# Equal FFN column groups, and gate logits through DRAM, in a fused attention and expert kernel

## The chip, the cores and the metric

The kernel runs on one core of one Trainium2 chip. The metric is the device time of one execution in microseconds (us). Each version was run several times. A profiled execution also gives a trace, whose span (first to last instruction) is some 1.7 us shorter than the time of the same execution. Engine names in the profile: PE is TensorE, PEld its weight loads, DVE VectorE, ACT ScalarE, POOL GpSimd, SP SyncE; SPq is SyncE issuing DMAs.

## The reference, cut to what matters

x is 2048 tokens of 1024, in bf16. Branch A is a linear attention of 32 heads with phi(t) = max(t, 0) + min(exp(t), 1), up to a tiny constant. Branch B adds a gated FFN's output to one token, the one with the highest router score. Both are mixed by a gate per token.

```python
x = A_x
g = sigmoid((x * gate_w).sum(-1, keepdims=True))    # one gate per token
a = linear_attention(x, wqkv) @ wo                  # branch A
r = x @ w_r
i = argmax(r)                                       # one token of 2048
y = (silu(x[i] @ w_gate) * (x[i] @ w_up)) @ w_down  # F = 3584 units
b = x;  b[i] += y * sigmoid(r[i])                   # branch B
return g * a + (1 - g) * b
```

## The kernel before

The main loop, for token tiles 4 to 15, makes keys and values (`unit_KV`), accumulates them (`unit_KVACC`) and makes queries (`unit_Q`). These units, all but the accumulation, go through the same four buffers (`ps_work`) in PSUM, the memory that TensorE writes to. ScalarE and VectorE empty (evacuate) keys and queries by `phi_evac`; values are copied out by ScalarE. The router runs before this loop, and the FFN's pieces are spread over it.

One matmul group gives router scores and gate logits of all tokens, one row of each per block of 512 tokens. `rg_f` is its copy in SBUF: gate logits in partitions 1, 33, 65 and 97. Two steps of the loop matter here: four small matmuls (eight records in the trace) move the logits to token columns, and the FFN's 3584 columns are made in halves of four and three groups of 512, each in its own 32 columns of the TensorE array.

```python
ps_work = ctx.enter_context(tc.tile_pool(name="ps_work", bufs=4, space=PSUM))
# issued on SyncE, in this order, ahead of the loop
nc.sync.dma_start(out=wq[:], in_=wqkv_v[:, :, 0:D])
nc.sync.dma_start(out=xp[:], in_=x2d)       # copy of x in DRAM; row i is overwritten later
# ...
def phi_evac(ps, out_ap):
    e0 = tmp.tile([P, 512], F32, tag="phi_e0")
    last_act[0] = nc.scalar.activation(e0[:], ps, ACTF.Exp)
    e1 = tmp.tile([P, 512], F32, tag="phi_e1")
    nc.vector.tensor_scalar(e1[:], e0[:], 1.0, EPS, op0=ALU.min, op1=ALU.add)
    nc.vector.scalar_tensor_tensor(out_ap, ps, 0.0, e1[:], op0=ALU.max, op1=ALU.add)
# ...
rg_f = rt.tile([P, 512], F32)
nc.scalar.copy(rg_f[:], rps[:])
# ... VectorE finds the candidates of the four blocks: cand
nc.gpsimd.dma_start(out=c4[:], in_=cand[0:128:32, :])            # "c" in the trace
# ... VectorE reduces c4 to the token's index: idx_f, idx_i
nc.gpsimd.dma_start(out=xsel_row[:], in_=x2d[bass.ds(idx_val, 1), :])

def router_part2():                          # called at t == 5
    # ... eight matmuls xs_ps <- xsel_row
    gl_ps = ps_ffn.tile([P, NT], F32, tag="f")
    for b in range(4):
        nc.tensor.matmul(gl_ps[:, 4 * b : 4 * b + 4], lhsT=rg_f[:, b * P : (b + 1) * P], rhs=selg[:], start=True, stop=True)
    nc.scalar.activation(gate[...], gl_ps[...], ACTF.Exp, scale=-1.0)
    # ... gate = 1 / (1 + gate), omg = 1 - gate
# ... ffn_pieces, for each half, matrix and c (8 chunks of 128 rows)
wt = ffw.tile([P, 2048], BF, tag="ffw")      # ten of these in flight
nc.sync.dma_start(out=wt[:, 0 : 512 * nr], in_=wv[:, c, c0 : c0 + 512 * nr])
for j in range(nr):                          # nr = 4, then 3
    nc.tensor.matmul(ps[32 * j : 32 * j + 32, :], lhsT=xs_pad[:, c, :], rhs=wt[:, 512 * j : 512 * j + 512],
                     start=(c == 0), stop=(c == KC - 1), tile_position=(0, 32 * j))
```

`pin_act`, which the kernel uses at two other places, adds an ordering-only dependency on the latest evacuation, so that the scheduler can't move an operation ahead of it on ScalarE.

Of the kernel before, what the change touches and what calls it, by code (L numbers as in the profile page):

```python
# [11 lines left out]
F32 = mybir.dt.float32  # L12
I32 = mybir.dt.int32
U32 = mybir.dt.uint32
ALU = mybir.AluOpType
ACTF = mybir.ActivationFunctionType
# [3 lines left out]
P = 128  # L20
# [3 lines left out]
NT = S // P  # L24
# [11 lines left out]
def kernel(  # L36
# [13 lines left out]
    nc = tc.nc  # L50
# [5 lines left out]
    const = ctx.enter_context(tc.tile_pool(name="const", bufs=1))  # L56
    keep = ctx.enter_context(tc.tile_pool(name="keep", bufs=1))
    dram = ctx.enter_context(tc.tile_pool(name="dram", bufs=1, space=DRAM))
    ps_work = ctx.enter_context(tc.tile_pool(name="ps_work", bufs=4, space=PSUM))
    ps_ffn = ctx.enter_context(tc.tile_pool(name="ps_ffn", bufs=1, space=PSUM))  # L60

    pq_all = keep.tile([P, NG, S], BF)
    gate = keep.tile([P, NT], F32)
    omg = keep.tile([P, NT], F32)
# [59 lines left out]
    nc.gpsimd.memset(one_bf[:], 1.0)  # L124
    sel4 = const.tile([P, 4], BF)
    nc.gpsimd.memset(sel4[:], 0.0)
    selg = const.tile([P, 4], F32)
    nc.gpsimd.memset(selg[:], 0.0)
    for j in range(4):
        nc.gpsimd.memset(sel4[32 * j : 32 * j + 1, j : j + 1], 1.0)  # L130
    pidx_i = const.tile([P, 4], I32)
    nc.gpsimd.iota(pidx_i[:], pattern=[[-32, 4]], base=-1, channel_multiplier=1)
    pidx_f = const.tile([P, 4], F32)
    nc.vector.tensor_copy(pidx_f[:], pidx_i[:])
    nc.vector.tensor_scalar(selg[:], pidx_f[:], 0.0, None, op0=ALU.is_equal)
    off16_i = const.tile([P, 1], I32)
    nc.gpsimd.iota(off16_i[:], pattern=[[0, 1]], base=0, channel_multiplier=16)
    off16 = const.tile([P, 1], F32)
# [3 lines left out]
    xs_pad = rt.tile([P, KC, 32], BF)  # L142
# [98 lines left out]
    nc.vector.tensor_copy(r_bf[:], rps[:])  # L241
    rg_f = rt.tile([P, 512], F32)
    nc.scalar.copy(rg_f[:], rps[:])
    r_f = rt.tile([P, 512], F32)
    nc.vector.tensor_copy(r_f[:], r_bf[:])
    mx8 = rt.tile([P, 8], F32)
# [27 lines left out]
    def router_part3():  # L274
        pin_act(nc.scalar.activation(sig[:], sig[:], ACTF.Exp, scale=-1.0))
        nc.vector.tensor_scalar_add(sig[:], sig[:], 1.0)
        nc.vector.reciprocal(sig[:], sig[:])

    def router_part2():
        xs_ps = ps_ffn.tile([P, KC], F32, tag="f")  # L280
        for c in range(KC):
            nc.tensor.matmul(xs_ps[:, c : c + 1], lhsT=xsel_row[0:1, c * P : (c + 1) * P], rhs=one_bf[0:1, 0:1],
                             start=True, stop=True)
        nc.vector.tensor_copy(xs_pad[:, :, 0], xs_ps[:])
        gl_ps = ps_ffn.tile([P, NT], F32, tag="f")
        for b in range(4):
            nc.tensor.matmul(gl_ps[:, 4 * b : 4 * b + 4], lhsT=rg_f[:, b * P : (b + 1) * P], rhs=selg[:], start=True, stop=True)  # L287
        nc.scalar.activation(gate[:].rearrange("p (j b) -> p j b", b=4), gl_ps[:].rearrange("p (b j) -> p j b", j=4),
                             ACTF.Exp, scale=-1.0)
        nc.vector.tensor_scalar_add(gate[:], gate[:], 1.0)  # L290
        nc.vector.reciprocal(gate[:], gate[:])
        nc.vector.tensor_scalar(omg[:], gate[:], -1.0, 1.0, op0=ALU.mult, op1=ALU.add)


    ffw = ph1.enter_context(tc.tile_pool(name="ffw", bufs=FFN_DEPTH))
    h_bf = [rt.tile([P, 512], BF, name=f"h_bf{i}") for i in range(2)]
    sg_t = [rt.tile([P, 512], F32, name=f"sg{i}") for i in range(2)]
# [1 line left out]

    def ffn_pieces():  # L300
        for half in range(2):
            nr = 4 if half == 0 else 3
            c0 = 2048 * half
            for wi, wmat in enumerate((B_w_gate, B_w_up)):
                wv = wmat.rearrange("(c p) f -> p c f", p=P)
                for c in range(KC):
                    def load(half=half, nr=nr, c0=c0, wv=wv, c=c):
                        wt = ffw.tile([P, 2048], BF, tag="ffw")
                        nc.sync.dma_start(out=wt[:, 0 : 512 * nr], in_=wv[:, c, c0 : c0 + 512 * nr])
                        return wt  # L310

                    def compute(wt, half=half, nr=nr, wi=wi, c=c):
                        if c == 0:
                            ps = ps_ffn.tile([P, 512], F32, tag="f")
                            ffn_state["ps"] = ps
                            if nr < 4:
                                nc.vector.memset(ps[96:128, :], 0.0)
                        ps = ffn_state["ps"]
                        for j in range(nr):
                            nc.tensor.matmul(ps[32 * j : 32 * j + 32, :], lhsT=xs_pad[:, c, :], rhs=wt[:, 512 * j : 512 * j + 512],  # L320
                                             start=(c == 0), stop=(c == KC - 1), tile_position=(0, 32 * j))
                        if c == KC - 1:
                            if wi == 0:
                                eg = tmp.tile([P, 512], F32, tag="ffn_e", bufs=1)
                                nc.scalar.activation(eg[:], ps[:], ACTF.Exp, scale=-1.0)
                                nc.vector.tensor_scalar_add(eg[:], eg[:], 1.0)
                                nc.vector.reciprocal(eg[:], eg[:])
                                nc.vector.tensor_tensor(sg_t[half][:], ps[:], eg[:], op=ALU.mult)
                            else:
                                nc.vector.tensor_tensor(h_bf[half][:], ps[:], sg_t[half][:], op=ALU.mult)  # L330

                                def h_transpose(half=half, nr=nr):
                                    hps = ps_ffn.tile([P, 16], F32, tag="f")
                                    for b in range(4):
                                        nc.tensor.matmul(hps[:, 4 * b : 4 * b + 4], lhsT=h_bf[half][:, b * P : (b + 1) * P],
                                                         rhs=sel4[:], start=True, stop=True)
                                    dst = hT_pad[:, 16 * half : 16 * half + 4 * nr, 0].rearrange("p (j b) -> p j b", b=4)
                                    src = hps[:].rearrange("p (b j) -> p j b", j=4)[:, 0:nr, :]
                                    nc.vector.tensor_copy(dst, src)

                                ffn_state["pending"] = h_transpose
                                ffn_state["barrier"] = True

                    yield load, compute
        wdv = B_w_down.rearrange("(k p) n -> p k n", p=P)
        for k2 in range(14):
            def load(k2=k2):
                wt = ffw.tile([P, 2048], BF, tag="ffw")
                nc.sync.dma_start(out=wt[:].rearrange("p (k n) -> p k n", k=2), in_=wdv[:, 2 * k2 : 2 * k2 + 2, :])
                return wt  # L350

            def compute(wt, k2=k2):
                if k2 == 0:
                    ffn_state["ps"] = ps_ffn.tile([P, 256], F32, tag="f", name="yps")
                ps = ffn_state["ps"]
                for kk in range(2):
                    k = 2 * k2 + kk
                    for j in range(4):
                        nc.tensor.matmul(ps[32 * j : 32 * j + 32, :], lhsT=hT_pad[:, k, :],  # L359
                                         rhs=wt[:, 1024 * kk + 256 * j : 1024 * kk + 256 * j + 256],  # L360
                                         start=(k == 0), stop=(k == 27), tile_position=(0, 32 * j))
                if k2 == 13:
                    brow = rt.tile([P, 256], BF, name="brow")
                    nc.vector.scalar_tensor_tensor(brow[:], ps[:], sig[:, 0:1], xsel4[:], op0=ALU.mult, op1=ALU.add)  # L364
                    nc.gpsimd.dma_start(out=xp[bass.ds(idx_val, 1), :].rearrange("o (j n) -> (o j) n", j=4),  # L365
                                        in_=brow[0:128:32, :])

            yield load, compute
# [4 lines left out]
    def ffn_prefetch():  # L373
        while len(inflight) < FFN_DEPTH:
            nxt = next(pieces, None)
            if nxt is None:
                return
            inflight.append((nxt[0](), nxt[1]))
# [16 lines left out]
                return  # L395

    ffn_prefetch()

    q_units = deque((g, j) for j in range(4) for g in range(NG))
    for t in range(4):  # L400
        unit_KVACC(t)
    for t in range(4, NT):
        for nb in range(4):
            unit_KV(t, nb)
            if nb == 1 and t > 4:
                unit_KVACC(t - 1)
        nq = Q_PER_T[t]
        for _ in range(nq):
            unit_Q(*q_units.popleft())
        if t == 5:  # L410
            router_part2()
        if t == 8:
            router_part3()
        if t >= 6:
            ffn_step(FFN_PER_T[t])
    unit_Q(*q_units.popleft())
# [145 lines left out]
```

## Time and profile before

| | before |
|---|---|
| median of 3 runs (range) | 267.6 us (267.37 to 267.88) |
| span of the profiled execution | 267.3 us |
| TensorE busy | 255.7 us, 96% |
| DMA moved | 47.71 MB, 33058 packets |
| SyncE: first FFN load issued, last issued | 30.68, 52.93 us |

The page's first lines stand in the prediction below. Two more views say what TensorE's time is made of. First the shares of the chain that ended last, from the page; then two rows of the groups of instructions, by form (line, engine, operation, tiles, shape, count, then busy us and mean ns of one, then idle time before them):

```profile
PE 77%; DVE 12%; DMA 7%; issue 2%; ACT 0%; POOL 0%; SPq 0%; DVEq 0%
```

```profile
L287 PE MATMUL gl_ps<-selg,rg_f 128*128 128x4 f32 x8 | 1.0, 253 | 0.1
L320 PE MATMUL ps<-wt,xs_pad 128*32 128x512 bf16 x112 | 7.6, 380 | 0.0
```

The chain is mostly TensorE. The two rows hold nearly all the TensorE work that the change touches. The second row also shows why means mislead: 112 matmuls of 380 ns would be 42.6 us, but three or four run beside each other and the group is busy for 7.6.

### The profile page before, as it was taken

Reading aid. Unit: us, or ns where it says so; the run is one execution under the profiler, and the core shown is the slowest. Engines: PE = TensorE matmul, PEld = TensorE weight load, DVE = VectorE, ACT = ScalarE, POOL = GpSimd, SP = SyncE. Lnnn points to the kernel's source line nnn. Section 1 sums busy time; section 2 is a strip of 40 time slices with the busy share of each in tenths; the row PEclk is TensorE's granted clock in tenths of the full one; section 3 lists DMA queues with packets and bytes.
Section 4 is the critical chain, followed back from the end, with each engine's and each line's share of the span. In section 5 each row is a group of like instructions: output and inputs, shape, how many; then the busy total and the mean of one; then the engine's idle time right before and its main releaser. Section 6 shows DMA issues by size and latency. Waiting matters only on the chain.

```text
span 267.3 us, 3972 instructions
## 1 busy us (share of the span) xinstructions
PE 255.7 (96%) x1510; PEld 121.8 (46%) x1537; DVE 144.5 (54%) x278; ACT 89.3 (33%) x138; POOL 50.3 (19%) x102
## 2 busy tenths in 40 slices
PE   7799999599999999999999999999999899999994
PEld 4444455245444445444444455544444344444443
DVE  4355014452375533539433425279999889984443
ACT  1433332123233322332322331233576623333310
POOL 7000001120000000000000000111969317990000
PEclk9999999999999999999999999999999999999999
DMA  6999998892078048019319608084000336455222
GB/s 228 359 312 220 246 521 306 292 415 93 0 259 333 1 154 316 4 45 348 120 36 357 238 0 300 17 286 168 1 1 2 125 100 197 150 170 177 86 78 78
DMA packets 33058, 47.71 MB, mean 178 GB/s; under 512 B 14152, under 2 KB 18640, under 8 KB 32976
## 3 DMA queue, kind: packets, MB, share of 16 engines
q1 hardware_dynamic: 32688, 47.32, 53.0%
q8 instruction: 12, 0.20, 0.3%
q0 software_dynamic: 320, 0.14, 0.2%
q14 instruction: 6, 0.05, 0.0%
q10 hardware_dynamic: 32, 0.00, 0.0%
HBM read 39.85 MB, written 8.39 MB: 180 GB/s over the span
## 4 chain that ended last, share of the span: by engine, by line
PE 77%; DVE 12%; DMA 7%; issue 2%; ACT 0%; POOL 0%; SPq 0%; DVEq 0%
PE ps L195 39%; PE ps L519 19%; PE ps L211 11%; DVE rb L476 4%; DVE e L169 3%; DMA c<-cand 3%; PE ps L320 3%; DVE pq_all L170 2%; DMA wkv<-in_A_wqkv_dram 2%; PE kvacc L204 2%; DMA rdp<-rd 1%; PE yps L359 1%; PE rps L237 1%; PE dps L453 1%; PE gl_ps L287 0%
## 5 line engine op out<-in xcount | busy, mean ns | idle before, releaser
L195 PE MATMUL ps<-wkv,xT 128*128 128x512 bf16 x498 | 113.9, 379 | 2.2 <-DMA wkv<-in_A_wqkv_dram 1.0
L195 PEld LDWEIGHTS <-xT 128*128 128x128 bf16 x512 | 48.8, 98 | 58.4 <-issue 2.9
L167 ACT ACTIVATE e<-ps 128x512 f32<-128x512 f32 x64 | 38.2, 597 | 81.7 <-PE ps L195 43.3
L169 DVE TENSOR_SCALAR e<-e 128x512 f32<-128x512 f32 x64 | 31.4, 492 | 55.7 <-ACT e L167 55.5
L211 PE MATMUL ps<-xT,wq 128*128 128x512 bf16 x248 | 58.3, 379 | 3.3 <-DVE idx_i L265 2.8
L519 PE MATMUL ps<-m_sb,pq_all 128*128 128x512 bf16 (+1 forms) x259 | 55.3, 372 | 1.0 <-DVE pq_all L170 0.6
L211 PEld LDWEIGHTS <-wq 128*128 128x128 bf16 x256 | 24.8, 98 | 33.6 <-issue 4.6
L519 PEld LDWEIGHTS <-pq_all 128*128 128x128 bf16 x264 | 25.7, 98 | 31.3 <-issue 1.8
L478 POOL TENSOR_TENSOR pq_all<-pq_all,rb 128x512 bf16<-128x512 bf16 x32 | 37.3, 1197 | 9.9 <-DVE rb L476 9.8
L200 ACT CAST vt<-ps 128x512 bf16<-128x512 f32 x32 | 18.8, 587 | 41.5 <-PE ps L195 41.5
L521 DVE SCALAR_TENSOR_TENSOR ot<-ps,gate,xg 128x512 bf16<-128x512 f32 (+1 forms) x33 | 23.8, 734 | 14.2 <-PE ps L519 14.1
L513 ACT ACTIVATE xg<-xt,omg 128x1024 f32<-128x1024 bf16 x16 | 18.2, 1151 | 29.7 <-DVE ot L521 25.0
L476 DVE STREAM_SHUFFLE rb<-rdp 128x512 f32<-128x512 f32 x32 | 22.7, 743 | 0.0
L170 DVE SCALAR_TENSOR_TENSOR pk<-ps,e 128x512 bf16<-128x512 f32 x32 | 22.1, 691 | 1.1
L170 DVE SCALAR_TENSOR_TENSOR pq_all<-ps,e 128x512 bf16<-128x512 f32 x32 | 21.8, 683 | 0.6
L192 POOL MEMSET vt<- 128x8 bf16 x16 | 1.9, 135 | 106.4 <-PE kvacc L204 106.4
L204 PEld LDWEIGHTS <-pk 128*128 128x128 bf16 x128 | 8.5, 98 | 3.3 <-issue 0.4
L204 PE MATMUL kvacc<-vt,pk 128*128 128x129 bf16 x128 | 9.7, 221 | 0.0
L484 ACT CAST m_sb<-ps 128x512 bf16<-128x512 f32 x16 | 8.6, 593 | 0.0
L458 DVE RECIPROCAL rd<-dn 128x512 f32<-128x512 f32 x2 | 6.7, 3353 | 3.2 <-ACT dn L456 3.2
L241 DVE CAST r_bf<-rps 128x512 bf16<-128x512 f32 x1 | 0.7, 691 | 13.9 <-PE rps L237 13.9
L365 POOL DMA_DIRECT2D xp<-brow x1 | 0.6, 575 | 38.5 <-DVE brow L364 38.5
(97 smaller groups left out, 87.0 us busy)
## 6 DMA issues: line engine op xcount, KB each, us to landing
wt<-in_B_w_down_dram SPq DMA_DIRECT2D x14, 512.0 KB, 9.2
wkv<-in_A_wqkv_dram SPq DMA_DIRECT2D x4, 1024.0 KB, 10.6
wt<-in_B_w_gate_dram SPq DMA_DIRECT2D x8, 512.0 KB, 21.6
wt<-in_B_w_up_dram SPq DMA_DIRECT2D x8, 512.0 KB, 8.1
xt<-xp SPq DMA_DIRECT2D x16, 256.0 KB, 2.7
out_dram<-ot SPq DMA_DIRECT2D x15, 256.0 KB, 2.0
wt<-in_B_w_gate_dram SPq DMA_DIRECT2D x8, 384.0 KB, 6.2
wt<-in_B_w_up_dram SPq DMA_DIRECT2D x8, 384.0 KB, 6.8
```

What stands on the lines that cost most here:

```text
L167: last_act[0] = nc.scalar.activation(e0[:], ps, ACTF.Exp)
L169: nc.vector.tensor_scalar(e1[:], e0[:], 1.0, EPS, op0=ALU.min, op1=ALU.add)
L170: nc.vector.scalar_tensor_tensor(out_ap, ps, 0.0, e1[:], op0=ALU.max, op1=ALU.add)
L195: nc.tensor.matmul(ps[:], lhsT=xT[:, c, t * P : (t + 1) * P], rhs=wkv[:, c, 512 * nb : 512 * nb + 512], start=(c == 0), stop=(c == KC - 1))
L200: nc.scalar.copy(vt_t[t][:, 4 * (nb - 2) : 4 * (nb - 2) + 4, 0:128], ps[:].rearrange("p (g e) -> p g e", g=4))
L204: nc.tensor.matmul(kv_slot(g), lhsT=pk_t[t][:, g * P : (g + 1) * P], rhs=vt_t[t][:, g, :], start=False, stop=False, skip_group_check=True)
L211: nc.tensor.matmul(ps[:], lhsT=wq[:, c, g * P : (g + 1) * P], rhs=xT[:, c, 512 * j : 512 * j + 512], start=(c == 0), stop=(c == KC - 1))
L476: nc.vector.stream_shuffle(rb[:], rd[:], [8 * (j % 2) + g] * 32)
L478: nc.gpsimd.tensor_tensor(sl, sl, rb[:], op=ALU.mult)
L513: pin_act(nc.scalar.activation(xg[:], xt[:], ACTF.Copy, scale=omg[:, t : t + 1]))
L519: nc.tensor.matmul(ps[:, 0:cw], lhsT=pq_all[:, g, t * P : (t + 1) * P], rhs=m_sb[:, g, c0 : c0 + cw], start=(g == 0), stop=(g == NG - 1))
L521: nc.vector.scalar_tensor_tensor(ot[:, c0 : c0 + cw], ps[:, 0:cw], gate[:, t : t + 1], xg[:, c0 : c0 + cw], op0=ALU.mult, op1=ALU.add)
```

## The change

It has two aims: equal FFN groups, so that the second half doesn't leave a quarter of the array's columns unused, and no TensorE work for the gate logits. 3584 columns become four groups of 896 = 512 + 384. The logits are written to DRAM as four rows of 2 KB and read back as 2048 single elements, token by token, into the columns where they are needed. The source calls the gate computation at tile 10 rather than at tile 5.

```diff
+    gl_d = dram.tile([4, 512], F32, name="gl_d")
+    gl = rt.tile([P, NT], F32)
+    def gate_logits():                       # called after the first ten FFN loads
+        nc.sync.dma_start(out=gl_d[:], in_=rg_f[1:128:32, :])
+        with nc.allow_non_contiguous_dma(reason="2048 gate logits to token columns"):
+            nc.sync.dma_start(out=gl[:].rearrange("p (j b) -> p j b", b=4), in_=gl_d[:].rearrange("j (b p) -> p j b", p=P))
+    def gates():                             # called at t == 10
+        nc.scalar.activation(gate[:], gl[:], ACTF.Exp, scale=-1.0)
+        nc.vector.tensor_scalar_add(gate[:], gate[:], 1.0)
 ... (reciprocal and 1 - gate as before; selg, gl_ps and their set-up removed)
-            nr = 4 if half == 0 else 3
-            c0 = 2048 * half
+            w = 512 if half == 0 else 384
+            c0 = 512 * half
-                        nc.sync.dma_start(out=wt[:, 0 : 512 * nr], in_=wv[:, c, c0 : c0 + 512 * nr])
+                        nc.sync.dma_start(out=wt[:, 0 : 4 * w].rearrange("p (j f) -> p j f", j=4),
+                                          in_=wv[:, c, :].rearrange("p (j f) -> p j f", j=4)[:, :, c0 : c0 + w])
-                        for j in range(nr):
-                            nc.tensor.matmul(ps[32 * j : 32 * j + 32, :], lhsT=xs_pad[:, c, :], rhs=wt[:, 512 * j : 512 * j + 512],
+                        for j in range(4):
+                            nc.tensor.matmul(ps[32 * j : 32 * j + 32, 0:w], lhsT=xs_pad[:, c, :], rhs=wt[:, w * j : w * j + w],
 ... (silu, product and transpose of the hidden units on w columns)
```

## The prediction

> **What bounds the kernel now.** I read the page first, then the chain of waits in order of time, then the timelines of ScalarE, TensorE and the DMA issues around 50 us, then the DMA landings. The page says TensorE is the bound:
>
> ```profile
> span 267.3 us, 3972 instructions
> PE 255.7 (96%) x1510; PEld 121.8 (46%) x1537; DVE 144.5 (54%) x278; ACT 89.3 (33%) x138; POOL 50.3 (19%) x102
> PE   7799999599999999999999999999999899999994
> ```
>
> So work taken off TensorE shortens the span, and an engine that stops feeding it lengthens it. The one dip inside (slice 7, 46.8 to 53.5 us) is the router: VectorE waits in order for a small transfer (c), and TensorE runs out of PSUM buffers. The chain shows this and what follows (start, us, work):
>
> ```profile
> 42.39 8.13 DMA c<-cand
> ...
> 52.44 1.88 PE ps L211 x8
> 54.32 0.65 PE ps L195 x3
> ...
> 57.77 0.47 PE kvacc L204 x8
> 58.24 3.45 PE ps L195 x16
> ...
> 64.08 1.03 PE gl_ps L287 x8
> ...
> 73.80 1.84 PE ps L320 x32
> ...
> 117.67 1.84 PE ps L320 x24
> ...
> 159.81 1.64 PE yps L359 x56
> ```
>
> The reader is to see three things. From 52.44 us on TensorE runs without a gap. The gate-logit matmuls cost it 1.03 us. In the FFN, 32 matmuls of 512 columns on four column groups take the same 1.84 us as 24 on three: a step costs as long as its longest group, not the sum.
>
> ScalarE's timeline and the DMA issues at that time:
>
> ```profile
> 49.62 0.60 ACT L167 ACTIVATE e<-ps 128x512 f32<-128x512 f32 x1 [1.14 <-PE ps L211]
> 54.35 0.60 ACT L167 ACTIVATE e<-ps 128x512 f32<-128x512 f32 x1 [4.13 <-PE ps L211]
> 65.15 0.18 ACT L288 ACTIVATE gate<-gl_ps 128x16 f32<-128x16 f32 x1 [1.09 <-PE gl_ps L287]
> ```
>
> ```profile
> 50.32 0.33 SPq L309 DMA_DIRECT2D wt<-in_B_w_gate_dram  x1
> 51.64 1.62 SPq L309 DMA_DIRECT2D wt<-in_B_w_up_dram  x2
> ```
>
> ```profile
> wt<-in_B_w_up_dram SPq DMA_DIRECT2D x1, 512.0 KB, 10.2
> ```
>
> Ten FFN weight loads of 0.52 MB stand in the SyncE queue behind the 4 MB copy of x, which lands at 50.3 us (issued 29.88, 20.4 us). Loads nine and ten are issued at 51.64 and 52.93 and land 10.2 us later, so at 61.8 and 63.1. They are paced by what is queued ahead of them: 10 x 0.52 MB from 50.3 to 63.1 us is 410 GB/s, and the windows show the same:
>
> ```profile
> 12.00:14.00 2.00, 1.43 (x13) 0.86 (x12) 1.72 (x3) 1.19 (x2) 0.00 (x0) 1.00 1.09 348
> 54.00:56.00 2.00, 1.95 (x10) 0.92 (x10) 0.98 (x2) 0.60 (x1) 0.00 (x0) 1.00 1.02 414
> ```
>
> The last column is GB/s. The first window moves key/value weights in rows of 1 KB (512 bf16), the second FFN weights in rows of 4 KB.
>
> **What the Trainium skill says.** "TensorE: Matmul & The Clock Gate", section "Architectural detail", says that ScalarE and VectorE execute strictly first in, first out. The trace agrees: VectorE stood 5.9 us before the reduction of c with evacuations behind it. The same page, "Part 1: The HAM clock gate", says that TensorE falls to half clock after an idle window of about 3.4 us and needs one such busy window to recover. Here the 8 matmuls that open the kernel take 3.6 us, twice the warm 1.73, while after the 2.8 us idle at 49.6 the next 8 take 1.88: no fall yet. "DMA: Bandwidth & Descriptors", "Queues, rings and completion order", says that one queue's descriptors are consumed in ring order on each DMA engine; the even 10.2 us above agree. Its "Rules for kernel authors" say that a strided last dimension becomes one descriptor per element; the trace of before has no such large transfer.
>
> **The change part by part.** I compared the compiled instruction order of both kernels.
>
> (a) Gate-logit matmuls gone: -1.03 us of TensorE.
>
> (b) FFN's second half: four groups of 384 columns in place of three of 512. Per step, 512 columns take 1.84/8 = 0.230 us, 256 columns (the down projection) 1.64/14 = 0.117. Linear between them, 384 take 0.174. Eight steps save 8 x 0.056 = 0.45 us; two matrices, 0.90 us. One hidden-transpose matmul of eight goes: 0.24/4 = 0.06. Total of (a) and (b): -2.0 us. The VectorE savings (two memsets of 0.49, a quarter off a 3.35 us reciprocal and its companions) lie on an engine that waits for TensorE here, so count 0.
>
> (c) FFN weight rows become 1 KB and 768 B. The ten prefetched loads then move at about 348 GB/s (the 12 to 14 us window) in place of 412: 5.24 MB / 348 = 15.1 us from 50.3, so until 65.4. By itself this is hidden: their first use is at 73.8.
>
> (d) The bounce. In the compiled order of SyncE, the write of the logits to DRAM follows the ten loads, and the gather with its 2048 four-byte elements follows the write. The write waits for the third weight load through a shared completion semaphore, about 50.3 + 3 x 1.5 = 54.8 us, and then stands in the rings behind the other seven. It lands about 65.8. The gather is issued then. Per DMA engine it has 2048/16 = 128 elements; the three DMA transposes move 12288 packets of 256 B, 768 per engine, in some 11 us, or 15 ns each, and I double that for scattered 4-byte reads and writes: 3.8 us, plus 1.7 us of fixed time (the last 64 KB stores land in 1.6). Landing: about 71.5 us. Both figures are estimates.
>
> (e) Who waits. The source calls the gate computation at token tile 10, but the scheduler moved it. In the compiled ScalarE order the exponential of the gates stands straight after the evacuation that ran at 49.62 in the trace, ahead of the one at 54.35. On VectorE the gate's add stands before the last step of that same first Q evacuation. Both are in order, so both stop until the gather lands. TensorE keeps going while buffers last. Its four working PSUM buffers rotate: the second Q unit and two key/value units still get theirs (52.44 to 57.77), then 0.47 of accumulation, and the unit that started at 58.24 needs the buffer of the first Q unit, whose evacuation is stuck. TensorE stops at 58.24.
>
> It resumes one gate exponential, one add and one evacuation after the landing: in before, 65.15 to 66.13 for the same three, so 1.05 with the semaphores. That is 71.5 + 1.05 = 72.55, an idle stretch of 14.3 us. Everything after it is bound by TensorE or starts from it, so I expect nothing to absorb it.
>
> (f) Cold restart: 14.3 us is far over the clock window. At the start of before the half rate lasted about 5 us (8 matmuls, then 16 transposes in 1.91 us against 0.46 for 8 warm ones), costing half, so +2.2 us.
>
> **Sum.** -2.0 + 14.3 + 2.2 = +14.5 us; 267.6 + 14.5 = 282.1 us.
>
> **The rivals.**
>
> *Only the work counts.* If the gather landed before about 57 us, or the gates ran at tile 10 as written, nothing would stall: 267.6 - 2.0 = 265.6 us, within 2%. Against it: the gates' exponential is in ScalarE's compiled order at about 50.2 us, before the write to DRAM can even be issued.
>
> *The bounce overtakes the weight loads.* Four descriptors of 2 KB might slip past. Then the write lands at about 57, the gather at 62.5, TensorE resumes at 63.6: idle 5.3, perhaps a cold start of 1.5, total about 272.4. For it: xsel_row, on another queue, landed in 4.5 us under the same load. Against it: this one is on the loads' own rings.
>
> *The gather is slow.* If an element costs 60 ns rather than 30, it takes 7.7 us in place of 3.8 and the total is 286.
>
> *The router's wait changes.* The transfer of c lands at 50.52, just after the copy of x at 50.3, which stands ahead of everything changed; I expect the 2.8 us dip unchanged. The row of x for the router lands at 62.9, needed at 63.35; a delay there disappears inside the new stall.
>
> **Range and chances.** The terms that matter are the landing of the write (63.5 to 67), the gather (3.5 to 10 us) and the cold restart (1 to 3). Their ends don't all fall together: 275 to 288 us, centre 282. To stay within 2% (below 272.9) the gather would have to land before about 62.5 us; I give that 0.07, and 0.02 to faster.
>
> **What would show it.** Right: ScalarE's largest wait is for the transfer of the gathered logits; TensorE idle once more, from about 58 us for 10 to 18 us; slow matmuls for some microseconds after; no gate-logit matmuls; second-half FFN steps of 0.17 us; the gap c at 49.6 to 52.4 unchanged; from there to the end the same order, shifted. Wrong: no wait on the gather, or an idle stretch under 5 us, or later stages that take the delay back.

## The result, and the profile after

The changed kernel took 278.82 us, median of 4 runs (277.88 to 280.01), beside 267.74 us for the kernel before (4 runs, 267.37 to 269.25). The ratio is 1.0405, 95% interval 1.0346 to 1.0464: slower. The page of the changed kernel, its lines for span, busy time, TensorE in 40 slices and granted clock:

```profile
span 276.1 us, 3986 instructions
PE 255.3 (92%) x1518; PEld 121.1 (44%) x1544; DVE 142.0 (51%) x274; ACT 88.9 (32%) x138; POOL 50.2 (18%) x100
PE   7899999722999999999999999999999899999995
PEclk9999999985899999999999999999999999999999
```

TensorE is busy as long as before (255.3 to 255.7), though it has less to do: some of its work ran at half clock, as the 5 and 8 of the last line show. The dip of slice 7 is now three slices wide. The chain of waits through it and on (start, us, work):

```profile
38.44 8.39 SPq L306
...
56.56 6.57 DMA gl_d<-rg_f
...
63.20 2.80 DMA gl<-gl_d
...
66.03 0.22 ACT gate L246
...
66.27 0.18 DVE gate L247
66.45 0.60 DVE pq_all L163
...
67.09 5.30 PE ps L188 x16
72.39 1.73 PE ps L204 x8
...
105.49 1.84 PE ps L316 x32
...
127.48 1.42 PE ps L316 x32
```

Read it from the bottom up. The 16 matmuls at 67.09 us start when one evacuation (pq_all) has freed a buffer. It stood behind the gate's add, which stood behind the gate's exponential, which waited for the gather of the logits (gl), which was issued when the write of them (gl_d) had landed. That write was issued at 56.56, at the end of ten FFN loads in SyncE's own stream: one of these alone held the issuing for 8.39 us. The timelines of ScalarE and then of TensorE name the two waits (in brackets: us idle before, and what ended it):

```profile
66.03 0.21 ACT L246 ACTIVATE gate<-gl 128x16 f32<-128x16 f32 x1 [15.99 <-DMA gl<-gl_d]
```

```profile
56.20 0.64 PE L197 MATMUL kvacc<-vt,pk 128*128 128x129 bf16 x8
67.09 5.30 PE L188 MATMUL ps<-wkv,xT 128*128 128x512 bf16 x16 [10.25 <-DVE pq_all L163]
```

ScalarE waited 16.0 us and TensorE 10.25: the buffers covered the first part. A table of windows gives the clock (columns: stretch and its length, then busy us and count of PE, PEld, DVE, ACT and POOL, then granted clock, DMA share, GB/s):

```profile
58.00:60.00 2.00, 0.00 (x0) 0.00 (x0) 0.00 (x0) 0.00 (x0) 1.77 (x4) 1.00 1.11 350
60.00:62.00 2.00, 0.00 (x0) 0.00 (x0) 0.00 (x0) 0.00 (x0) 0.00 (x0) 0.57 1.06 332
68.00:70.00 2.00, 2.00 (x6) 0.64 (x5) 1.86 (x5) 0.00 (x0) 0.00 (x0) 0.50 0.00 0
70.00:72.00 2.00, 2.00 (x9) 0.87 (x8) 0.65 (x1) 0.59 (x1) 0.00 (x0) 0.87 0.00 0
```

A clock of 0.57 over 2 us is 0.28 us at 1 and the rest at 0.5, so the clock fell at about 60.28, which is 3.44 us after TensorE stopped at 56.84. By the same sum 0.87 puts its return at about 70.5, which is 3.4 us after work began again. (Both sums take the clock to be either full or half, as it is in the windows around them.) The 16 matmuls took 5.30 us in place of the 3.45 of before: 1.85 us lost. The last column shows the narrow FFN rows at 350 GB/s, where the wide ones ran at 414.

The two traces side by side, as the start of the same work in each:

| landmark | before | changed | difference |
|---|---|---|---|
| second query unit starts (after the wait for c) | 52.43 | 51.03 | -1.40 |
| the next key/value unit gets a buffer | 58.24 | 67.09 | +8.85 |
| that unit and its pair done | 61.69 | 72.39 | +10.70 |
| next key/value unit after the router's matmuls | 65.11 | 74.77 | +9.66 |
| denominators start | 176.12 | 185.05 | +8.93 |
| first output matmul | 212.12 | 220.97 | +8.85 |
| end of the span | 267.3 | 276.1 | +8.8 |

So the whole loss arises between 52 and 72 us: -1.40 from a shorter wait for c, +10.25 idle, +1.85 at half clock. The saved gate-logit matmuls give 1.04 back and the FFN's second half 0.73; nothing later takes the delay back or adds to it. The medians differ by 11.1 us rather than 8.8: the profiled execution of the changed kernel was the fastest of its four (277.88), while that of the kernel before took 269.0, above its median. Only this one execution of the changed kernel has a trace, so how long the stall was in the other three isn't shown; their spans reach 278.4 us, and their mean granted clocks go down to 0.975, from 0.98 in the profiled one.

### The profile page after: what moved, and what is told of

The parts are those of the page before. It is cut to its first block, busy times and chain, and to the rows that moved or that the text cites. A ratio compares the mean times of both kernels' runs of the same rounds, so it can differ in the third digit from the quotient of the medians.

```text
span 276.1 us, 3986 instructions
## 1 busy us (share of the span) xinstructions
PE 255.3 (92%) x1518; PEld 121.1 (44%) x1544; DVE 142.0 (51%) x274; ACT 88.9 (32%) x138; POOL 50.2 (18%) x100
## 4 chain that ended last, share of the span: by engine, by line
PE 69%; DVE 10%; SPq 10%; DMA 7%; issue 2%; ACT 0%; POOL 0%; DVEq 0%
PE ps L188 35%; PE ps L519 19%; PE ps L204 10%; SPq L306 9%; DVE rb L476 4%; DVE e L162 3%; DVE pq_all L163 2%; DMA gl_d<-rg_f 2%; PE ps L316 2%; DMA wkv<-in_A_wqkv_dram 2%; PE kvacc L197 2%; DMA rdp<-rd 1%; PE yps L356 1%; DMA gl<-gl_d 1%; PE dps L453 1%
## 5 line engine op out<-in xcount | busy, mean ns | idle before, releaser
L188 PE MATMUL ps<-wkv,xT 128*128 128x512 bf16 x499 | 115.5, 383 | 12.6 <-DVE pq_all L163 10.3
```

The lines of the kernel that those rows point to most:

```text
L188: nc.tensor.matmul(ps[:], lhsT=xT[:, c, t * P : (t + 1) * P], rhs=wkv[:, c, 512 * nb : 512 * nb + 512], start=(c == 0), stop=(c == KC - 1))
```

## The experiments

My theory: the loss is the wait of in-order ScalarE and VectorE for the gather, plus the cold clock that follows; the FFN split itself is worth a little. The rivals: the narrower FFN rows cause the loss (they slow the queue that the write stands in); the bounce is slow whatever waits for it; the loss is spread over later stages. The runs came in three sessions, each on one chip, with its own runs of the kernel before: median 268.58 us for the first four experiments, 269.40 for the next four, 267.97 for the last two. All gave correct results. Ratios are to the kernel before of the same session.

| run | median us | ratio (95% interval) | span us |
|---|---|---|---|
| changed kernel | 278.82 | 1.0405 (1.0346 to 1.0464) | 276.1 |
| late gates | 267.34 | 0.9961 (0.9924 to 0.9998) | 264.8 |
| split only | 271.65 | 1.0109 (1.0067 to 1.0151) | 269.3 |
| bounce only | 278.51 | 1.0372 (1.0337 to 1.0406) | 276.5 |
| filled stall | 276.65 | 1.0299 (1.0263 to 1.0335) | 274.9 |
| split only, early wo | 270.92 | 1.0081 (1.0027 to 1.0134) | 268.9 |
| gates one tile later | 267.79 | 0.9952 (0.9903 to 1.0002) | 266.1 |
| bounce from GpSimd | 269.32 | 1.0019 (0.9967 to 1.0071) | 266.6 |
| late gates, late copy of x | 265.03 | 0.9853 (0.9806 to 0.9901) | 262.6 |
| before, late copy of x | 265.98 | 0.9919 (0.9878 to 0.9959) | 263.9 |
| early gates, late copy of x | 266.38 | 0.9937 (0.9894 to 0.9979) | 263.8 |

### Late gates: only the place of the gates in ScalarE's order

```diff
     def gates():                             # still called at t == 10
-        nc.scalar.activation(gate[:], gl[:], ACTF.Exp, scale=-1.0)
+        pin_act(nc.scalar.activation(gate[:], gl[:], ACTF.Exp, scale=-1.0))
```

> The changed kernel with the gates' exponential held in ScalarE's order at token tile 10, where the source calls it; nothing else moves. Theory A (ScalarE and VectorE stand in order behind the gather, TensorE runs out of PSUM buffers): the 10.25 us idle stretch and the half-clock matmuls after it vanish, leaving before minus the TensorE work taken away, 267.7 - 2.0 = 265.7 us (264.5 to 266.5). Theory B (the loss is DMA traffic: four times as many weight rows and a 2048-element gather slow what feeds TensorE): the time stays at 275 us or more, since all transfers are the same.

The stall is gone, with both parts of the change still in: 267.34 us, 11 less than the changed kernel. The exponential now runs at 117.0 us, as the source asks, and waits for nothing; the 16 matmuls that stalled follow the accumulation at 56.15 us at once. The exponential, then TensorE's timeline:

```profile
L246 ACT ACTIVATE gate<-gl x1: 207/207/207, 117.0 to 117.0; 128x16 f32<-128x16 f32 x1
```

```profile
56.62 3.62 PE L188 MATMUL ps<-wkv,xT 128*128 128x512 bf16 x16
```

So neither the bounce nor the narrow rows cost 11 us; the place of one small instruction does. The gain over the kernel before, though, is about 1.1 us (0.39% of 268.6) where I expected 2.0, and 267.34 lies above the range that I gave. TensorE's own waits show where some of it went:

```profile
PE ps L204 <- DVE idx_i L272: 1.6, 1, 1.6
PE xs_ps L289 <- DMA xsel_row<-in_A_x_dram: 1.1, 1, 1.1
```

The wait for c (first line) is 1.6 us, shorter than before. The second wait is new: the row of the chosen token lands too late for its matmuls. In the changed kernel it is hidden in the stall.

### Split only and bounce only: each part alone

Split only takes the bounce out and puts the gate-logit matmuls back. Bounce only puts the FFN's groups of before back, with rows of 4 KB.

```diff
 # split only
-    gate_logits()                            # and gates() with it
+    gl_ps = ps_ffn.tile([P, NT], F32, tag="f")   # selg, matmuls and activation as before
 # bounce only
-            w = 512 if half == 0 else 384
+            nr = 4 if half == 0 else 3       # loads, matmuls and transposes as before
```

> The column split alone, with the gate-logit matmuls of before. Theory A: no gather, no wait; the narrow rows are hidden, and only the second-half FFN steps shrink: 267.7 - 0.96 = 266.7 us, with 1.4 us per pass of 32 matmuls in place of 1.84 for 24. Theory B (narrow rows cost): several us slower than before, 270 us or more, with TensorE waiting for weights or the router's transfer.

> The DRAM bounce alone, with the FFN columns and 4 KB weight rows of before. Theory A: the stall is there again: the write of the logits is issued near 54.5 us behind seven wide loads, lands near 63.3, the gather 2.8 us later, TensorE resumes near 67.2, idle about 9 us, half clock costs 1.9, the gate-logit matmuls save 1.03: 276 to 279 us. If the narrow rows made most of the stall by slowing the queue: idle under 5 us and a time below 273 us.

Bounce only costs 3.7% on its own; the narrow rows are not needed for the loss, and that rival is out. ScalarE's and TensorE's timelines of it:

```profile
64.63 0.22 ACT L246 ACTIVATE gate<-gl 128x16 f32<-128x16 f32 x1 [14.57 <-DMA gl<-gl_d]
```

```profile
65.70 6.46 PE L188 MATMUL ps<-wkv,xT 128*128 128x512 bf16 x16 [8.43 <-DVE pq_all L163]
```

The write was issued at 53.20 here, 3.4 us earlier than in the changed kernel, but stood longer in its queue, and the gather was issued at 61.57. The idle stretch is 1.8 us shorter, and the half clock then costs more: 6.46 us for the 16 matmuls, 3.0 over the warm 3.45. By the windows it came back to full only at 71.5 us, 5.8 us after work began; in the changed kernel that took 3.4.

Split only missed: expected 266.7, measured 271.65, that is 1.1% slower than before. Its FFN steps do take 1.41 us, so the saving is there. Against it stand 0.84 us of TensorE waiting for the chosen row, and a longer last stage before the output: from the denominators to the first output matmul 38.2 us (175.71 to 213.91) where before has 36.0. There TensorE waited 1.8 us and VectorE 2.9, for the reciprocals of the denominators (rdp). In its chain:

```profile
181.62 6.34 DMA rdp<-rd
```

In the kernel before, the chain goes through another of these four transfers, which took 3.62 us. The DMA issues show one difference just ahead: the write of the FFN's result row took 3.7 us to land here, and 1.6 before, in the changed kernel and in late gates. The load of wo, which follows it, was issued at 174.88 in place of 173.23, so that the transfer of the reciprocals met more of it. That is a guess about a cause, and the next run tests it.

### Split only, early wo: is it the late load of wo?

```diff
-                    brow = rt.tile([P, 256], BF, name="brow")
+                    brow = keep.tile([P, 256], BF, name="brow")
```

The result row now lives in a pool that stays open, so wo needn't wait for its write.

> The column split alone again, with the routed row's result kept in a buffer that outlives the first phase, so that the load of the output weights (wo) no longer waits for that row's 3.7 us landing. The split alone took 271.65 us against 268.58 where I expected 1 us less than before; its trace puts 0.8 us on a wait for the routed row of x at 64 us and about 2.7 us on a late wo load (174.9 us against 173.2), which the reciprocals' transfer at 181 us then ran into (6.3 us to land in place of 3.6). If that is the cause: wo is issued near 172.5 us, the reciprocals land in under 4 us, and the time is 267 to 269 us. If the loss has another cause (the narrow rows themselves): 271 us or more.

It missed as well: 270.92 us, where 267 to 269 was expected. wo was issued at 173.04 and the last reciprocals landed in 3.07 us, so that much was undone. But the result row still took 3.7 us; the scheduler also moved two shuffles that need the reciprocals ahead of an evacuation, and VectorE and TensorE each waited 1.0 us. The stage took 37.27 us. So the late wo was part of the excess at most. Why the result row lands late in just these two kernels stays open; the changed kernel shows neither it nor a longer last stage (35.92 us).

### Filled stall: the stall without the cold clock

```diff
             if nb == 1 and t > 4:
                 unit_KVACC(t - 1)
+                if t == 5:
+                    fill_ps = ps_ffn.tile([P, 512], F32, tag="f")
+                    for _ in range(48):
+                        nc.tensor.matmul(fill_ps[:], lhsT=warm_sb[:, 0:P], rhs=warm_sb[:], start=True, stop=True)
```

48 useless matmuls keep TensorE busy just where it stops, with the wait for the gather left in.

> The changed kernel with 48 matmuls of 512 columns on a spare bank (48 x 0.216 = 10.4 us) put at the point where TensorE stops, so that it is never idle there. Theory: the clock stays full, the 16 matmuls after the stall take 3.45 us in place of 5.30, and the time falls by 1.85 us: about 277.0 us against 278.8 (up to 0.5 us more if the filler overruns the landing). Rival (the slow matmuls are caught up in later slack, or are slow for another reason): no change, 278.8 us or more.

TensorE's timeline of it:

```profile
56.65 10.52 PE L408 MATMUL fill_ps<-warm_sb 128*128 128x512 bf16 x48
67.66 3.61 PE L188 MATMUL ps<-wkv,xT 128*128 128x512 bf16 x16 [0.48 <-DVE pq_all L163]
```

The wait stays, ScalarE's is 16.6 us, and the 16 matmuls behind it take 3.61 us, which is their warm speed (3.62 in this view of before). The mean granted clock is 1.0 in all four runs, where the changed kernel's four had 0.975 to 0.981. The median is 2.2 us below the changed kernel's, and by the ratios of the two sessions 1.06% or 2.8 us: the cold clock is worth 2 to 3 us, the wait the rest.

### Gates one tile later, and the bounce from GpSimd: how late is late enough?

The first pins the gates as in late gates, but calls them at tile 5, just behind the query units. The second issues both transfers on GpSimd's queue, which doesn't stand behind the FFN loads, with the gates pinned at tile 4, one evacuation later than the scheduler had put them; so it alters two things.

```diff
 # gates one tile later
+        if t == 5:
+            gates()                          # pinned
 # bounce from GpSimd; gates() pinned at t == 4
-        nc.sync.dma_start(out=gl_d[:], in_=rg_f[1:128:32, :])
+        nc.gpsimd.dma_start(out=gl_d[:], in_=rg_f[1:128:32, :])   # and the gather too
```

> The changed kernel with the gates' exponential held only a few evacuations later, behind the Q evacuation of token tile 5, where ScalarE would arrive near 63 us. Theory A: the gather lands near 66.0 us as in the changed kernel, so ScalarE waits 2 to 3 us, less than the four rotating PSUM buffers cover (6.9 us); TensorE has no idle stretch over 1 us from it, its clock stays full, and the time is that of the late gates, 267.3 us (266.3 to 268.5). If any wait of ScalarE on the gather passed on to TensorE in full: about 2.5 us more, 269.8 us.

> The changed kernel with both transfers of the bounce issued from GpSimd, so on another queue than the weight loads, and the gates early in ScalarE's order again (one Q evacuation later than in the changed kernel). Theory: the landing is late because the write stands in the rings behind the loads; on its own queue it lands with the router's transfer near 49 us and the gather near 54, ScalarE waits little and TensorE not at all beyond the dip of before: 266.5 to 268.5 us. Rival: the gather itself is what is slow (2048 elements under load, or generated slowly by GpSimd), landing after 60 us: then TensorE stalls again and the time is 272 us or more.

ScalarE's timelines, first gates one tile later, then bounce from GpSimd:

```profile
68.34 0.22 ACT L246 ACTIVATE gate<-gl 128x16 f32<-128x16 f32 x1 [3.42 <-DMA gl<-gl_d]
```

```profile
58.98 0.22 ACT L246 ACTIVATE gate<-gl 128x16 f32<-128x16 f32 x1 [3.76 <-DMA gl<-gl_d]
```

In both ScalarE still waits, for 3.4 and 3.8 us, and in neither does TensorE stop for it: the four buffers last that long. Gates one tile later runs like late gates. Bounce from GpSimd missed: it is level with before, in ratio, and took 269.32 us where I expected 266.5 to 268.5. Its two small transfers landed 8.9 us after their issue each, under the load of everything else, so that the gather came at 59 us and not at the 54 I had counted on. That was early enough, but TensorE's waits for c (2.90 us) and for the chosen row (0.84) were there too.

### Late copy of x: does the wait for c follow the big copy?

All the kernels so far have a gap before the second query unit, where c lands 0.2 to 0.3 us after the 4 MB copy of x. Nothing needs that copy until much later. The edit takes it out of the place ahead of the FFN loads and makes it in four parts of 1 MB, each behind a later load.

```diff
-    nc.sync.dma_start(out=xp[:], in_=x2d)
+    def copy_x(i):
+        cp = nc.sync.dma_start(out=xp[512 * i : 512 * i + 512, :], in_=x2d[512 * i : 512 * i + 512, :])
+        tc.add_manual_dep(cp.ins, last_load[0].ins.name, NOSYNC, reason="keep the copy of x late in the SP queue")
 ...
             ffn_step(FFN_PER_T[t])
+        if t in (6, 8, 10, 12):
+            copy_x((t - 6) // 2)
```

It was added to late gates, then to the kernel before alone, then to the changed kernel with its gates where the scheduler puts them (here one evacuation earlier still).

> The late gates, and the 4 MB copy of x taken out of the queue before the FFN loads and made in four parts between later loads. Theory: the router's transfer c lands late (6.9 us) because it waits for the copy's 64 KB descriptors; without them it lands in 4 to 5 us, the dip of TensorE near 49 us (1.6 us) vanishes, and the routed row's wait (1.1 us) shrinks too: 1.5 to 2.7 us less than the late gates, 264.6 to 265.8 us. Rival: c waits for whatever is queued, loads as well as the copy: no change, 267.3 us; or the copy then slows the FFN loads and TensorE waits for weights: 268 us or more.

> The kernel before with nothing changed but the copy of x made late in four parts. It separates what the late copy gives by itself from what the change gives. Theory: the dip of 2.8 us at 49.6 us shrinks to about 0.6 as in the late-copy run, so 2 us less than before (ratio 0.992), and the change with late gates adds its 2 us of TensorE work to reach the 0.985 of that run. If the late copy gives the whole of it, the ratio here is 0.985 to 0.988 and the change itself is worth nothing.

> The changed kernel with the gates left early in ScalarE's order (the scheduler puts them one evacuation earlier still, before the first Q evacuation, near 47 us), and only the copy of x made late. Theory: the wait is as in the changed kernel but the queue is shorter by 4 MB, so the write of the logits lands near 52.4 us and the gather near 55.3; TensorE needs the stuck buffer near 55.8 and gets it near 57.3: idle about 1.5 us and no half clock, 1 to 2 us more than the 265.0 us of late gates with late copy, ratio to before 0.988 to 0.994. If the early wait costs TensorE in full (8 us) the ratio is above 1.01.

TensorE's timeline of late gates with the late copy, then that of early gates with it:

```profile
50.02 1.89 PE L203 MATMUL ps<-xT,wq 128*128 128x512 bf16 x8 [0.62 <-DVE idx_i L271]
```

```profile
57.13 3.61 PE L187 MATMUL ps<-wkv,xT 128*128 128x512 bf16 x16 [1.26 <-DVE pq_all L162]
```

All three times came out as expected, though c took more than the 4 to 5 us that I had given it: it lands in 5.9 us, where late gates had 6.9, and the gap is 0.62 us. In before with the late copy c lands in 5.3 us and TensorE doesn't wait there at all. Late gates with the late copy is the fastest kernel, 265.03 us, 1.5% below before with an interval that leaves 1 out but doesn't reach 2% as a whole. Most of it isn't the change's: the copy alone makes the kernel before 0.8% faster, which leaves about 0.7 points for the change with its gates late. The two intervals overlap, and the runs are of two sessions, so that rest isn't clear of noise. Part of what the copy gives may be the clock: of the 21 runs of before in the three sessions, 7 had a mean granted clock of 0.993 or 0.994 (269.2 us in the mean, the others 268.4), while none of the 12 runs with the late copy lay under 0.999. In the last run the gates stand early, but the write no longer has the copy ahead of it: the gather was issued at 52.1 us, ScalarE waited 6.8 us and TensorE 1.26, short of any cold clock. So the stall needs two things at once: a consumer early in the order, and a transfer late in the queue. Removing either one removes nearly all of it.

## Why the prediction was right

The time was foretold at 282.0 us (275 to 288) and came at 278.82. By the steps of the sum:

- **TensorE work saved, -2.0: right.** The gate-logit matmuls are gone, worth 1.04 us in the trace (1.03 predicted). An FFN step of the second half takes 1.42 and 1.41 us per eight chunks where 8 x 0.174 = 1.39 was expected; with the transpose, 0.73 of the 0.96 appear between the landmarks.
- **The scheduler's order decides, and the gates stand early: right.** The exponential ran directly behind the evacuation at 49.44 us, and late gates, whose source alters only this, has no stall.
- **The stop point, 58.24: it came at 56.84,** since the wait for c was 1.63 us and not the unchanged 2.8. This was the wrong word on a rival: "I expect the 2.8 us dip unchanged". c follows the landing of the copy of x, which came at 48.84 rather than 50.3 in this trace. The late copy of x shows the link.
- **The landing of the write, 65.8: it came at 63.13.** The parts were wrong in opposite directions. It was issued at 56.56, not 54.8, because SyncE itself was held while it issued the narrow loads; the wait for the third load's semaphore, which I had named, doesn't show. But the copy of x had landed 1.4 us earlier, the loads were moving even before that (277 GB/s from 47.0 to 47.5 us), and their 350 GB/s was as predicted.
- **The gather, 5.5 us: it took 2.80.** This is the term mis-sized most. I had doubled the 15 ns per element of the DMA transposes; with the same 1.7 us of fixed time, 2.80 leaves 1.1 us for 128 elements of each engine, under 9 ns each. The transfer engines were nearly idle then: the windows show 36 GB/s and less around it.
- **Idle stretch, 14.3: it was 10.25.** From the gather's landing at 66.00 to TensorE's start took 1.09 us (1.05 predicted). What is missing is the gather's 2.7 us and the write's 2.7, less the 1.4 by which TensorE stopped sooner: -4.0.
- **Cold restart, 2.2: 1.85 in the changed kernel, 3.0 in bounce only.** (Half of the 5 us that the prediction names would be 2.5, so its 2.2 doesn't follow from its own lines.)
- **Narrow rows hidden by themselves: right in the changed kernel only.** I said that a delay of the chosen row "disappears inside the new stall", and it does. Without the stall TensorE waits 0.6 to 1.1 us for the row in late gates, both split-only kernels and bounce from GpSimd, all with narrow rows. That the rows delay it is argued: the row took 4.9 to 5.2 us to land in these, 4.5 in before, and 2.4 in late gates with the late copy, whose rows are narrow too.
- **Nothing absorbs it later: right.** The difference is 8.93 us at the denominators and 8.8 at the end.

So the mechanism was right, and the size lay at the low end: in the traces the loss is 8.8 us where the sum has 14.5, and the idle stretch of 10.25 is only just inside the 10 to 18 foretold. The two large errors, gather and write, have the same sign. That the median came nearer to 282 than the trace is no merit of the sum: the other three executions were 0.5 to 2.1 us longer than the profiled one, for reasons that no trace shows.

Of the rivals, the gather at 60 ns per element and the bounce overtaking the loads are both refuted by the chain. "Only the work counts" was nearly what late gates measured, at some 0.9 us less gain than its 2.0.

The parts don't add up: split only and bounce only lose 1.1 and 3.7%, together 4.8 where the changed kernel loses 4.05, but with these intervals the excess isn't clear of noise. The wait for the chosen row is hidden by the stall, and the longer last stage of split only doesn't occur in it. What makes that stage longer is not settled.

## What to carry to other kernels

Before moving a small computation onto a DMA's result, look where its consumer ends up in the compiled order of an in-order engine, not where the source calls it: 0.2 us of work stopped a 96% busy TensorE for 10 us, and an ordering-only pin cured it. The write of 8 KB landed only when the traffic of the loads ahead of it in its queue had died down (332 GB/s in the window before 62 us, 36 in the next, landing at 63.13), so a small urgent transfer belongs ahead of, or away from, prefetches and copies that nobody needs yet. Where one engine is 96% busy, taking 0.8% of its work away can gain 0.8% at most, which a single new wait eats up.

## What the Trainium skill lacked or had wrong

- "DMA: Bandwidth & Descriptors", section "Issuing engines are not separate DMA queues", calls the time that a sequencer needs to initiate a DMA usually small beside the DMA itself. Here one load of 512 KB in rows of 1 KB held SyncE's issuing for 8.39 us while the copy of x was in the queue, and ten loads took until 56.5 us to issue, against 53.2 with rows of 4 KB. That a limit on queued descriptors holds it is only argued.
- The same page, "Specifications", gives 512 B as the least transfer for full rate. Rows of 1 KB moved 350 GB/s here and rows of 4 KB 414, both at a DMA share over 1.
- The same page's "Rules for kernel authors" warns of strided last dimensions but gives no duration. 2048 four-byte elements landed 2.8 us after their issue from SyncE on otherwise idle transfer engines (3.0 with late gates and the late copy), and 8.9 us from GpSimd under load.
- "TensorE: Matmul & The Clock Gate", "Part 1: The HAM clock gate", has the clock fall after an idle window of about 3.4 us. The changed kernel agrees, with 3.44. But gates one tile later fell to half clock after an idle stretch of only 2.17 us, inside which no such window fits: 8 matmuls took 2.84 us in place of 1.89. Before's 2.8 us idle at the same place did not do this. By finer windows the clock fell at 52.38 us and came back at 55.80, 3.42 us later; in the changed kernel and in bounce only it was down for 10.24 us, three times 3.41. So in these three traces it changed in steps of about 3.4 us, and the step that ended with the fall at 52.38 held 1.24 us of TensorE work beside the 2.17 idle. A window that isn't wholly idle was enough here; how much work it may hold is open. The timeline of gates one tile later and a window of it:

```profile
51.60 2.84 PE L204 MATMUL ps<-xT,wq 128*128 128x512 bf16 x8 [2.17 <-DVE idx_i L272]
```

```profile
53.00:54.00 1.00, 1.00 (x4) 0.40 (x3) 0.00 (x0) 0.00 (x0) 0.00 (x0) 0.50 1.11 360
```

- None of the pages that I read warns that a scheduler may hoist a DMA-fed instruction in an in-order engine's stream. Its cost here was 16.0 us of waiting on ScalarE and 10.25 on TensorE.
